# Attention and two expert layers on one core: how value products and row sums are laid out on TensorE's columns

## The chip, the cores and the metric

The kernel runs on one core of one Trainium2 chip. Its engines are called PE (TensorE; PEld is its weight load), DVE (VectorE), ACT (ScalarE), POOL (GpSimd) and SP (SyncE, which issues the DMAs here). The metric is the device time of one execution in microseconds (us); a number of runs gives a median.

## The reference

Three stages follow each other. Attention over 2 batches, 8 heads, 768 positions and head size 64; a key takes part for a query only where both fall into the same of 64 buckets, which the signs of six projections give:

```
mask = q_bucket[:, :, :, None] == k_bucket[:, :, None, :]
scores = where(mask, scale * (q @ k.T), -1e9)
attn = exp(scores - max(scores))
attn = attn / (sum(attn) + 1e-9)
out = attn @ v
```

Then a feed-forward layer with Mish over 1536 tokens (512 to 2048 to 512), and then eight experts of width 1024, whose weights per token come from a softmax balanced by eight Sinkhorn rounds. Everything is float32. The change touches only the attention stage.

## The kernel before

Work in attention is cut into 32 units `u`, one for each head and half of its queries (384 of 768). A unit has six chunks `c` of 128 keys. Its steps:

- `s_mm` multiplies queries by keys, two matmuls for each of three groups of 128 queries, and `s_max` (DVE) takes the row maxima. `rows_mm` turns them into a row, which `rows_cp` and a DMA (`rows_move`) put beside the queries.
- `st_mm` makes the transposed scores of one chunk with two matmuls (lines 414 and 415), and `st_exp` (ACT, line 420) writes their exponentials into one of five tiles `p` (128 keys x 384 queries).
- `av_mm` (line 458) multiplies `p` by the values of this chunk. The stationary operand has 128 columns: 64 of values and 64 of ones, so one output tile `pav` holds the unnormalised output on 64 partitions and the sums on the other 64. Two columns more than 384 (`WIDE`) carry a tiny constant for rows without a match.
- A chunk is multiplied in one of two ways. In plain float32 it is one matmul in the program, which the trace shows as two PE instructions (`pav<-p,vt`). A *split* chunk goes through the rounded type fp32r: `split_hi` (ACT or DVE, line 423) rounds `p` into `ph`, `split_lo` (POOL, line 426) makes the rest `pl`, and three matmuls follow (`ph,vl`, `pl,vh`, `ph,vh`). Chunks 0, 1 and 3 of each unit but the first are split: 93 split chunks and 99 plain ones.
- `av_out` moves sums (DVE transpose, line 466) and output (ACT copy, line 468) out of PSUM, and `norm` divides two heads together and rounds the result into `xh` and `xl`, the input of the next stage.
- `bits_mm` (line 343) computes the projections of a head. It is the one place where matmuls stand on column groups: four matmuls of 32 output columns each write PSUM partitions 0, 32, 64 and 96. Head 0 alone uses two groups of 64 columns.

No engine's order is written by hand. A planner takes tasks with costs (`COST`), due times and dependences, gives each engine (`E` is PE, `A` ACT, `D` DVE, `P` POOL, `Q` the DMA queue) its next task by the earliest start plus a small weight on the due time, and emits the code in that order. While PE would idle at the start it adds filler matmuls (`keep_warm`).

The first steps of the later stage, the decoding of the int64 weights, are woven into attention on ACT, DVE and POOL. The feed-forward layer begins with line 796.

Of the kernel before, what the change touches and what calls it, by code (L numbers as in the profile page):

```python
# [16 lines left out]
P = 128  # L17
# [5 lines left out]
E = 8  # L23
# [8 lines left out]
TINY = float(2.0 ** -64)  # L32
# [4 lines left out]
NS = 3  # L37
NRAW = 1
NP = 5
NPH = 3  # L40
# [3 lines left out]
WHOLE = {0: (0, 1, 3, 4), **{u: (4,) for u in range(1, 32)}}  # L44
# [20 lines left out]
def lsh_attention_moe_kernel(  # L65
# [111 lines left out]
    def attention():  # L177
        with ExitStack() as a:
# [14 lines left out]
            homes = {(NH - 3 + x) % NS: x for x in range(NX)}  # L193
# [8 lines left out]
            vt = [sets.tile([P, NKC, 3, D], F32, name=f"vt{i}") for i in range(2)]  # L202

            SPLIT = [0, 1, 3, 4]
            splits = lambda u, c: c in SPLIT and c not in WHOLE.get(u, ())
            vh = [sets.tile([P, len(SPLIT), 3, D], F32R, name=f"vh{i}") for i in range(2)]
            vl = [sets.tile([P, len(SPLIT), 3, D], F32R, name=f"vl{i}") for i in range(2)]
# [3 lines left out]
            some = out_p.tile([P, HALF // 32], F32, name="some")  # L211
# [4 lines left out]
            phs, pls = ([p_p.tile([P, 512], F32R, name=f"{n}{i}") for i in range(NPH)] for n in ("ph", "pl"))  # L216
# [3 lines left out]
            row_t, s_t, st_t, p_t, ph_t, av_t = {}, {}, {}, {}, {}, {}  # L220

            split_order = [(u, c) for u in range(NU) for c in range(NKC) if splits(u, c)]
            parts_no = {x: n for n, x in enumerate(split_order)}
            used_m = [0]
# [25 lines left out]
            def load_v(h):  # L250
                nc.sync.dma_start(out=vt[h // 2 % 2][:, :, h % 2 * 2, :], in_=v[h])

            def clear(kind, i):
                e = nc.vector if (kind, i) in FAST else nc.gpsimd
                if kind == "sq":
                    e.memset(f32(sq[i][64:96]), 0.0)
                elif kind == "bk":
                    e.memset(f32(bk[i][64:96]), 0.0)
                elif kind == "one":
                    e.memset(f32(bk[i][96:97]), 1.0)  # L260
                elif kind == "vt":
                    e.memset(vt[i][:, :, 1, :], 1.0)
                elif kind == "vl":
                    e.memset(f32(vl[i])[:, :, 1, :], 0.0)
                elif kind == "vh":
                    e.memset(f32(vh[i])[:, :, 1, :], 1.0)

            def clear_slots(j):
                t, x = ((ps, TINY), (phs, TINY), (pls, 0.0))[j]
                for y in t:  # L270
                    nc.gpsimd.memset((f32(y) if j else y)[:, HALF:WIDE], x)
# [11 lines left out]
            def keep_warm(n):  # L283
                if nm(av_mm, 1, 0) in ends:
                    return
                if nm(st_mm, 0, 0) in ends and len(warm) == 1:
                    if nm(av_mm, 0, 0) in ends:
# [73 lines left out]
            def queries(u):  # L361
                half = u % 2
                return slice(half * HALF, (half + 1) * HALF)

            def s_mm(u, t):
                s, q0 = u // 2 % NS, u % 2 * HALF + t * P
# [31 lines left out]
            def rows_cp(u):  # L398
                m = row_t[u]
                n = 1 if u < DIRECT else 3  # L400
                if u < DIRECT:
                    dst, src = sq[u // 2 % NS][96:97, queries(u)], m[0:n, :HALF]
# [5 lines left out]
            def rows_move(u):  # L408
                move(sq[u // 2 % NS][96:97, queries(u)], row_t[u])

            def st_mm(u, c):
                s, q, k = u // 2 % NS, queries(u), slice(c * P, (c + 1) * P)
# [15 lines left out]
            def split_hi(u, c, e):  # L428
                ph_t[u, c] = phs[parts_no[u, c] % NPH]
                copy(e, ph_t[u, c][:, :HALF], p_t[u, c][:, :HALF])  # L430

            def split_lo(u, c, e):
                lo = pls[parts_no[u, c] % NPH]
                subtract(e, lo[:, :HALF], p_t[u, c][:, :HALF], f32(ph_t[u, c])[:, :HALF])
                p_t[u, c] = lo

            def split_v(h, j, e):
                b = h // 2 % 2
                src = vt[b][:, :, h % 2 * 2, :].rearrange("p (a b) d -> p a b d", b=3)[:, :, 0:2]
                hi, lo = (x[b][:, :, h % 2 * 2, :].rearrange("p (a b) d -> p a b d", b=2) for x in (vh, vl))  # L440
                if j == 0:
                    copy(e, hi, src)
                else:
                    subtract(e, lo, src, hi.bitcast(F32))

            def av_mm(u, c):
                h = u // 2
                b, k = h // 2 % 2, slice(h % 2, h % 2 + 2)
                p = p_t.pop((u, c))
                if c == 0:  # L450
                    av_t[u] = slot(ps_a, "a", u, 2, [P, 512], F32, "pav")
                if splits(u, c):
                    i, hi = SPLIT.index(c), ph_t.pop((u, c))
                    pairs = [(vl[b][:, i, k], hi), (vh[b][:, i, k], p), (vh[b][:, i, k], hi)]
                else:
                    pairs = [(vt[b][:, c, k], p)]
                for n, (x, y) in enumerate(pairs):
                    nc.tensor.matmul(  # L458
                        av_t[u][:, :WIDE], x.rearrange("p a d -> p (a d)"), y[:, :WIDE],
                        start=(c == n == 0), stop=(c == NKC - 1 and n == len(pairs) - 1),  # L460
                    )

            def av_out(u, j):
                q, t, o = queries(u), av_t[u], 64 * (u // 2 % 2)
                if j == 0:
                    nc.vector.transpose(out=rs[o:o + 64, q], in_=t[64 - o:128 - o, :HALF])
                else:
                    nc.scalar.copy(xu[o:o + 64, u % 2, :WIDE], t[o:o + 64, :WIDE])


            def norm(u, part, e=None):
                h, half = divmod(u, 2)
                b, hp = divmod(h // 2, H // 2)
                c, x = queries(u), xu[:, half, :HALF]
                g = slice(b * S + half * HALF, b * S + (half + 1) * HALF)
                if part == 0:
                    nc.gpsimd.tensor_scalar(
                        out=some, in0=rs[:, c].rearrange("p (b j) -> p b j", j=32)[:, :, 0],
                        scalar1=0.0, scalar2=1e-9, op0=ALU.is_gt, op1=ALU.mult,
                    )  # L480
                elif part == 1:
                    nc.vector.scalar_tensor_tensor(
                        out=nr, in0=rs[:, c].rearrange("p (b j) -> p b j", j=32)[:, :, 0],
                        scalar=S * TINY, in1=some, op0=ALU.max, op1=ALU.add,
                    )
                    nc.vector.reciprocal(out=nr, in_=nr)
                elif part == 2:
# [4 lines left out]
                elif part == 3:  # L492
                    nc.vector.scalar_tensor_tensor(
                        out=x, in0=x, scalar=xu[:, half, HALF:HALF + 1], in1=rs[:, c], op0=ALU.add, op1=ALU.mult
                    )
                elif part == 4:
# [7 lines left out]
            def task(engines, due, f, *args, after=(), cost=None, lag=0.01, ring=None, frees=None):  # L504
# [3 lines left out]
                "E": dict(warm_up=2.6, bits_mm=0.66, s_mm=0.355, rows_mm=0.13, st_mm=0.355),  # L508
                "A": dict(
                    av_out=0.47, load_table=0.2, prep_hi=0.83, prep_move=0.83, st_exp=0.49,  # L510
                    split_hi=0.51, split_v=0.4, norm=0.51, decode=0.68, weight_hi=1.05,
                ),
                "D": dict(
                    av_out=0.58, bits_cmp=0.47, clear=0.7, clear_start=0.85, proj_parts=0.7, gate_parts=0.45,
                    prep_lo=0.64, s_max=0.95, rows_cp=0.29, split_hi=0.5, split_v=0.42,
                    norm=0.6, decode=0.46,
                ),
                "P": dict(
                    clear=0.6, prep_lo=1.0, split_lo=1.0, split_v=0.73, norm=1.0, decode=1.3, weight_lo=1.27,
                ),  # L520
            }
            SHARED = {prep_lo, proj_parts, split_hi, split_v, decode, clear, clear_start, gate_parts}
# [3 lines left out]
            PICK = (prep_lo, split_hi, split_lo, split_v, norm, decode)  # L526
# [3 lines left out]
            def st_done(u):  # L530
                return [nm(st_mm, u, c) for c in range(NKC)] if u >= 0 else []

# [9 lines left out]
            for j in range(3):  # L542
                task("P", -20 + j, clear_slots, j, cost=0.18)
# [5 lines left out]
            for i in range(2):  # L549
                for kind in ("vt", "vh", "vl"):  # L550
                    task("P", -3 + 2 * i, clear, kind, i, after=[nm(hold)])


            for h in range(NH):
                due = 6 * (2 * h - 3)
                old = 2 * (h - NS) + 1
# [28 lines left out]
                prev = h - 4  # L585
                freed = [nm(av_mm, 2 * prev + 1, NKC - 1), nm(split_v, prev, 1)] if prev >= 0 else []
                vdue = 12 * h - 12 * (h % 2) - 10.0
# [745 lines left out]
```

## Time and profile before

| | us |
|---|---|
| median of 3 runs | 1512.87 (1512.62 to 1513.23) |
| span of the profiled execution | 1511.8 |
| PE busy in the span | 1503.5 |
| first matmul of the feed-forward layer | 246.16 |

The span is what the instructions of the profiled execution cover; its own time is not given beside it, and the median of the runs is 1.1 us longer. A timeline gives the start of each PE instruction and its length. PE instructions are pipelined: one of 384 columns is shown as 0.34 us long, while the next one starts 0.18 us after it. So what a matmul costs a full PE is read from start to start, not from its length. The trace merges equal instructions that follow each other (x2), and the granted clock of PE is 1.00 in all slices.

### The profile page before, as it was taken

The numbers are of one execution on the slowest core, as the hardware profiler recorded it, in microseconds if no ns is written. First come the engines' busy times: TensorE is split into PE (matmuls) and PEld (weight loads), VectorE is DVE, ScalarE is ACT, GpSimd is POOL, SyncE is SP. The second block draws the span as 40 slices with busy tenths as digits, with TensorE's granted clock in tenths as the row PEclk, the third lists the DMA queues.
The fourth block names the chain that finished last, engine by engine and source line by source line (L and its number), as shares of the span: only waits on it lengthen the run. The fifth ranks groups of instructions, "written<-read, shape, count | busy, mean of one in ns | idle before, by whom it ended". The sixth has DMA issues, their size and how long they took to land.

```text
span 1511.8 us, 20162 instructions
## 1 busy us (share of the span) xinstructions
PE 1503.5 (99%) x7435; PEld 1318.3 (87%) x7435; DVE 885.7 (59%) x1419; ACT 685.6 (45%) x1225; POOL 902.8 (60%) x759
## 2 busy tenths in 40 slices
PE   9999999999999999999999999999999999999998
PEld 6788888888887898999989899998989999898988
DVE  7999896777625567666444466753434535344353
ACT  6778776654333343344333334343333434333331
POOL 5778774443313586666666666666666666666660
PEclk9999999999999999999999999999999999999999
DMA  8455641222200131222222222232222222222211
GB/s 217 118 156 147 146 111 29 84 84 70 70 14 3 41 97 59 68 70 70 70 70 70 63 64 70 70 110 71 70 68 61 67 70 70 70 70 70 64 49 42
DMA packets 66490, 116.70 MB, mean 77 GB/s; under 512 B 18276, under 2 KB 20440, under 8 KB 66392
## 3 DMA queue, kind: packets, MB, share of 16 engines
q1 hardware_dynamic: 66392, 115.43, 25.8%
q8 instruction: 58, 0.95, 0.3%
q14 instruction: 40, 0.33, 0.1%
HBM read 93.41 MB, written 3.15 MB: 64 GB/s over the span
## 4 chain that ended last, share of the span: by engine, by line
PE 97%; DVE 2%; issue 0%; ACT 0%; DVEq 0%; ACTq 0%
PE y L1185 35%; PE u L1118 31%; PE y L821 9%; PE pav L458 7%; PE h L796 3%; PE h L797 3%; PE h L798 3%; PE ps L372 2%; PE pst L414 2%; PE pst L415 2%; DVE mx L386 1%; PE pbits L343 0%; PE lg L849 0%; PE warm L291 0%; PE prow L395 0%
## 5 line engine op out<-in xcount | busy, mean ns | idle before, releaser
L1126 ACT ACTIVATE gh<-c 128x384 fp32r<-128x384 f32 x256 | 134.6, 526 | 174.6 <-DVE c L1138 172.6
L1138 DVE TENSOR_TENSOR u<-u,p 128x384 f32<-128x384 f32 x64 | 35.7, 558 | 284.1 <-PE u L1118 282.2
L1131 DVE SCALAR_TENSOR_TENSOR gl<-c,gh 128x384 fp32r<-128x384 f32 x256 | 195.7, 827 | 0.0
L1185 PE MATMUL y<-ww,gh 128*128 128x512 f32 x768 | 186.6, 391 | 0.0
L1185 PE MATMUL y<-w,gh 128*128 128x512 f32 x768 | 186.0, 391 | 0.0
L1185 PEld LDWEIGHTS y<-w,gh 128*128 128x128 f32 x768 | 143.7, 188 | 28.9
L1185 PEld LDWEIGHTS y<-ww,gh 128*128 128x128 f32 x768 | 143.7, 188 | 28.8
L1001 POOL TENSOR_TENSOR w<-stage,w 128x1024 fp32r<-128x1024 f32 x32 | 76.3, 2386 | 89.1 <-ACT w L997 89.1
L426 POOL TENSOR_TENSOR pl<-p,ph 128x384 fp32r<-128x384 f32 x93 | 99.5, 1079 | 44.7 <-ACT ph L423 41.7
L1001 POOL TENSOR_TENSOR ww<-stage,ww 128x1024 fp32r<-128x1024 f32 x32 | 76.3, 2384 | 81.7 <-ACT ww L997 81.7
L420 ACT ACTIVATE p<-pst 128x384 f32<-128x384 f32 x192 | 93.5, 490 | 49.4 <-PE pav L458 26.5
L821 PE MATMUL y<-gh,w 128*128 128x512 f32 x336 | 109.8, 389 | 0.0
L151 POOL TENSOR_TENSOR stage<-stage,sgn 128x512 f32<-128x512 f32 x32 | 43.1, 1347 | 110.4 <-DVE sgn L149 100.4
L997 ACT CAST ww<-stage 128x1024 fp32r<-128x1024 f32 x32 | 33.6, 1052 | 157.5 <-PE y L1185 157.5
L997 ACT CAST w<-stage 128x1024 fp32r<-128x1024 f32 x32 | 33.6, 1050 | 154.5 <-PE y L1185 154.5
L386 DVE TENSOR_REDUCE mx<-ps 128x1 f32<-128x768 f32 x95 | 90.1, 949 | 18.8 <-PE ps L372 17.9
L977 POOL TENSOR_TENSOR wa<-stage,wa 128x512 fp32r<-128x512 f32 x32 | 45.6, 1424 | 89.0 <-ACT wa L972 80.0
L1185 PE MATMUL y<-ww,gl 128*128 128x512 f32 x384 | 98.2, 389 | 0.0
L1185 PE MATMUL y<-w,gl 128*128 128x512 f32 x384 | 97.6, 389 | 0.0
L977 POOL TENSOR_TENSOR wx<-stage,wx 128x512 fp32r<-128x512 f32 x32 | 45.4, 1419 | 80.5 <-ACT wx L972 80.5
L1118 PE MATMUL u<-tw,w 128*128 128x384 f32 x480 | 91.9, 336 | 0.0
L1118 PE MATMUL u<-tw,ws 128*128 128x384 f32 x480 | 91.7, 336 | 0.0
(218 smaller groups left out, 3843.4 us busy)
## 6 DMA issues: line engine op xcount, KB each, us to landing
stage<-in_w_dram SPq DMA_DIRECT2D x160, 512.0 KB
raw<-in_qk_dram SPq DMA_DIRECT2D x13, 384.0 KB
sb<-hi SPq DMA_DIRECT2D x18, 192.0 KB
vt<-in_v_dram SPq DMA_DIRECT2D x16, 192.0 KB
wx<-hi SPq DMA_DIRECT2D x16, 192.0 KB
out_dram<-acc SPq DMA_DIRECT2D x11, 256.0 KB
zq<-hi SPq DMA_DIRECT2D x10, 192.0 KB
ak<-hi SPq DMA_DIRECT2D x10, 192.0 KB
```

The costliest lines, as they stand in the source:

```text
L386: nc.vector.tensor_reduce(out=m[:, t:t + 1], in_=s_t[t][:, :, :HALF], axis=AX.XY, op=ALU.max, negate=True)
L420: nc.scalar.activation(p_t[u, c][:, :HALF], st_t.pop((u, c))[:, :HALF], AF.Exp, scale=0.125)
L426: (nc.gpsimd if e == "P" else nc.vector).tensor_sub(out, in0, in1)
L458: nc.tensor.matmul(av_t[u][:, :WIDE], x.rearrange("p a d -> p (a d)"), y[:, :WIDE], start=(c == n == 0), stop=(c == NKC - 1 and n == len(p ...
L821: nc.tensor.matmul(yps[j], x, y, start=(head and m == 0), stop=(tail and m == 2))
L977: nc.gpsimd.tensor_sub(a[:, 1, 0:512], t[:, 0, :], f32(a)[:, 0, 0:512])
L997: nc.scalar.copy(wbuf[u % 2]["w"][:, 0, :], staged["u", u, 1].rearrange("p c n -> p (c n)"))
L1001: nc.gpsimd.tensor_sub(y[:, 1, :], t, f32(y)[:, 0, :])
L1118: nc.tensor.matmul(bank[x], weight(u, a, m, kc), moving(u, b, mm, kc), start=(first and n == 0), stop=(n == 5), skip_group_check=not first)
L1126: nc.scalar.activation(hi, src, AF.Relu)
L1131: nc.vector.scalar_tensor_tensor(out=lo, in0=src, scalar=0.0, in1=f32(hid_u[u, c][0]), op0=ALU.max, op1=ALU.subtract)
L1185: nc.tensor.matmul(y_t[t], (hi, hi, lo)[m][:, t % 3 * P:(t % 3 + 1) * P], y, start=(k == 0 and first), stop=(k == NF // 2 - 1 and last),)
```

## The change

Both ways of multiplying a chunk are replaced by one. Heads 2k and 2k+1 are now handled together: `members(n)` names the two units of a pair, which have the same half of the queries, and for the first four units the order of heads and halves is changed (`head`, `half_of`). `av_mm` issues, for one chunk, two float32 matmuls with 64 stationary columns (values alone): the even head writes PSUM partitions 0 to 63, the odd head 64 to 127. For the first two pairs each unit's chunk is a task of its own (`av_one`).

The sums no longer come with the values. POOL adds chunks 0 and 1, and 2 and 3, of a unit (`add`), and `sum_mm` multiplies these sums and chunks 4 and 5 by ones, eight float32 matmuls of 32 output columns on four column groups for a pair. Each head's sum then lies in two parts on two partition groups; `norm` brings them together with an ACT copy and four small DMAs. `split_hi`, `split_lo`, `split_v` and `av_out` go. There are 14 tiles `p` in place of 5, a fourth set of operands (`NS`), and six tiles `pa`.

```diff
-NS = 3
-NP = 5
-NPH = 3
-WHOLE = {0: (0, 1, 3, 4), **{u: (4,) for u in range(1, 32)}}
+NS = 4
+NP = 14
+NPA = 6
+AVG = 1
+AVX = 0.1
+AVD = 6
+ADDS = "P"
...
-                if splits(u, c):
-                    i, hi = SPLIT.index(c), ph_t.pop((u, c))
-                    pairs = [(vl[b][:, i, k], hi), (vh[b][:, i, k], p), (vh[b][:, i, k], hi)]
-                else:
-                    pairs = [(vt[b][:, c, k], p)]
...
+            def add(u, g, e):
+                t = pa_t[u, g] = pas[(2 * u + g) % NPA]
+                (nc.gpsimd if e == "P" else nc.vector).tensor_add(t, p_t[u, 2 * g][:, :HALF], p_t[u, 2 * g + 1][:, :HALF])
+
+            def av_chunks(n, us, g):
+                if n not in av_t:
+                    av_t[n] = slot(ps_a, "a", n, 2, [P, 512], F32, "pav")
+                for c in range(AVG * g, AVG * g + AVG):
+                    for u in us:
+                        e = head(u) % 2
+                        nc.tensor.matmul(
+                            av_t[n][64 * e:64 * e + 64, :WIDE], vt[head(u) // 2 % 2][:, c, e, :], p_t[u, c][:, :WIDE],
+                            start=(c == 0), stop=(c == NKC - 1),
+                        )
...
+            def sum_mm(n):
+                sum_t[n] = next_m("psum")
+                for k in range(2):
+                    for u in members(n):
+                        for x in range(2):
+                            r = 64 * (head(u) % 2) + 32 * x
+                            nc.tensor.matmul(
+                                sum_t[n][r:r + 32, :HALF], ones[:, 0:32], p_t[u, 4 + x][:, :HALF] if k else pa_t[u, x],
+                                start=(k == 0), stop=(k == 1),
+                            )
+
+            def norm_move(n, x):
+                y = x ^ 1
+                nc.sync.dma_start(out=other[32 * x:32 * x + 32], in_=own[32 * y:32 * y + 32])
...
-                    task("E", i + 1.0, av_mm, u, c, cost=0.53 if sp else 0.65,
...
+                        task("E", 6 * part[-1] + AVG * g + AVD, f, x, g,
+                             after=[nm(st_exp, u, c) for u in part for c in range(AVG * g, AVG * g + AVG)] + ([nm(f, x, g - 1)] if g else room)
...
+                task("E", due + 8, sum_mm, n, after=[nm(add, u, g) for u in us for g in range(2)] + [nm(st_exp, u, c) for u in us for c in (4, 5)], ring="m", frees=nm(norm, n, 0))
...
+                    task("Q", due, norm_move, n, x, lag=0.3, after=[nm(norm, n, 1)])
```

On PE the planner's order is a new one throughout. In the middle of attention of the kernel before, between the score matmuls (`ps`, `pst`), PE has one matmul of a plain chunk and three of a split one, all with 128 output partitions (the numbers behind a name are those of buffers):

```order
L414 MATMUL pst<-wx_78 128x384
L415 MATMUL pst<-wx_78 128x384
L458 MATMUL pav<-p_140,vt_125 128x386
L458 MATMUL pav<-ph_141,vl_129 128x386
L458 MATMUL pav<-pl_144,vh_127 128x386
L458 MATMUL pav<-ph_141,vh_127 128x386
L414 MATMUL pst<-wx_78 128x384
L415 MATMUL pst<-wx_78 128x384
```

In the kernel after, PE has there two matmuls of 64 output partitions, one for each head of a pair, alone between score matmuls of 128:

```order
L442 MATMUL pav<-p_137,vt_128 64x386
L442 MATMUL pav<-p_143,vt_128 64x386
L399 MATMUL prow<-idt,mx_157 3x128
L376 MATMUL ps<-wx_78 128x384 x2
L418 MATMUL pst<-wx_78 128x384
L419 MATMUL pst<-wx_78 128x384
L418 MATMUL pst<-wx_78 128x384
L419 MATMUL pst<-wx_78 128x384
L442 MATMUL pav<-p_138,vt_128 64x386
L442 MATMUL pav<-p_144,vt_128 64x386
```

A few rows on, the sums of an earlier pair stand on PE, also between score matmuls:

```order
L419 MATMUL pst<-wx_78 128x384
L459 MATMUL psum<-pa_154,ones 32x384
L459 MATMUL psum<-pa_155,ones 32x384
L459 MATMUL psum<-pa_150,ones 32x384
L459 MATMUL psum<-pa_151,ones 32x384
L459 MATMUL psum<-p_140,ones 32x384
L459 MATMUL psum<-p_141,ones 32x384
L459 MATMUL psum<-p_146,ones 32x384
L459 MATMUL psum<-p_147,ones 32x384
L418 MATMUL pst<-wx_78 128x384
```

So the value products have moved from whole-width instructions among others of the same width to narrow ones. In the whole program of the kernel after they stand in 96 runs of neighbouring `pav` matmuls: 71 runs with one matmul on each of the two groups, 5 with two chunks and one with three chunks in a row on both groups, and 19 runs on one group only (14 single matmuls and 5 of two, all from the first two pairs). `psum` stands 16 times, `pbits` 16 times as before. In 12 places two of these narrow runs touch.

## Rows read from the trace of the kernel before

**Rows 1.** The page: busy time, and the chain that ended last.
```profile
PE 1503.5 (99%) x7435; PEld 1318.3 (87%) x7435; DVE 885.7 (59%) x1419; ACT 685.6 (45%) x1225; POOL 902.8 (60%) x759
...
PE 97%; DVE 2%; issue 0%; ACT 0%; DVEq 0%; ACTq 0%
PE y L1185 35%; PE u L1118 31%; PE y L821 9%; PE pav L458 7%; PE h L796 3%; PE h L797 3%; PE h L798 3%; PE ps L372 2%; PE pst L414 2%; PE pst L415 2%; DVE mx L386 1%; PE pbits L343 0%; PE lg L849 0%; PE warm L291 0%; PE prow L395 0%
```

**Rows 2.** Windows: stretch, its length, busy time and instructions of each engine, clock, DMA.
```profile
0.00:60.00 60.00, 55.84 (x294) 42.87 (x295) 47.54 (x79) 40.48 (x78) 34.89 (x58) 1.00 0.67 172
60.00:200.00 140.00, 139.69 (x745) 116.36 (x744) 126.49 (x192) 107.98 (x228) 106.81 (x108) 1.00 0.59 150
```

**Rows 3.** Timeline of PE, mid-attention: start, length, instruction, count.
```profile
152.66 0.34 PE L415 MATMUL pst<-sb 97*128 97x384 f32 x1
152.84 0.81 PE L458 MATMUL pav<-p,vt 128*128 128x386 f32 x2
153.19 0.63 PE L458 MATMUL pav<-ph,vl 128*128 128x386 f32 x1
153.66 0.34 PE L458 MATMUL pav<-pl,vh 128*128 128x386 f32 x1
153.84 0.33 PE L458 MATMUL pav<-ph,vh 128*128 128x386 f32 x1
154.01 0.34 PE L414 MATMUL pst<-zq,ak 128*128 128x384 f32 x1
```

**Rows 4.** Lines by shape to 247 us, PE: count, busy time, mean length in ns.
```profile
L458 PE MATMUL pav<-p,vt 128*128 128x386 f32 x198 | 80.0, 486 | 0.0
L458 PE MATMUL pav<-ph,vl 128*128 128x386 f32 x93 | 40.7, 437 | 0.0
L343 PE MATMUL pbits<-raw,pf 128*32 128x192 f32 x104 | 6.9, 338 | 0.0
L291 PE MATMUL warm<-xh 128*128 128x256 f32 x45 | 6.9, 292 | 0.0
```

**Rows 5.** Timeline of PE around one group of four narrow matmuls (eight instructions).
```profile
15.18 0.34 PE L414 MATMUL pst<-zq,ak 128*128 128x384 f32 x1
15.35 0.33 PE L415 MATMUL pst<-sb 97*128 97x384 f32 x1
15.62 0.53 PE L343 MATMUL pbits<-raw,pf 128*32 128x192 f32 x8
16.08 0.62 PE L372 MATMUL ps<-sb 96*128 96x384 f32 x2
16.53 0.34 PE L414 MATMUL pst<-zq,ak 128*128 128x384 f32 x1
```

**Rows 6.** Timeline of PE at its start: head 0's two groups of 64.
```profile
3.04 0.63 PE L281 MATMUL warm<-xh 128*128 128x512 f32 x1
...
3.46 0.63 PE L281 MATMUL warm<-xh 128*128 128x512 f32 x1
4.02 1.80 PE L343 MATMUL pbits<-raw,pf 128*64 128x384 f32 x4
5.76 0.58 PE L291 MATMUL warm<-xh 128*128 128x256 f32 x1
```

**Rows 7.** Timeline of PE: narrow matmuls on the first group alone.
```profile
466.57 0.39 PE L821 MATMUL y<-gh,w 128*128 128x512 f32 x1
466.79 1.10 PE L849 MATMUL lg<-xh,wgr 128*32 128x512 f32 x4
467.73 1.08 PE L849 MATMUL lg<-xl,wgr 128*32 128x512 f32 x4
468.64 0.40 PE L796 MATMUL h<-xh,wx 128*128 128x512 f32 x1
```

**Rows 8.** Lines by shape to 247 us, the other engines.
```profile
L426 POOL TENSOR_TENSOR pl<-p,ph 128x384 fp32r<-128x384 f32 x93 | 99.5, 1079 | 44.7 <-ACT ph L423 41.7 <-PE pav L458 1.8 <-DVE ph L423 0.7
...
L423 ACT CAST ph<-p 128x384 fp32r<-128x384 f32 x81 | 41.5, 513 | 2.4
```

**Rows 9.** Timeline of PE at the end of attention.
```profile
245.16 1.46 PE L458 MATMUL pav<-p,vt 128*128 128x386 f32 x4
246.16 0.69 PE L796 MATMUL h<-xh,w 128*128 128x512 f32 x1
```

More of the change, by code (lines that the diff above doesn't have):

```diff
@@ L191, in attention @@
             NU = 2 * NH
-            homes = {(NH - 3 + x) % NS: x for x in range(NX)}
+            homes = {(NH - NS + x) % NS: x for x in range(NX)}
             def part(i, j, name):
@@ L201, in attention @@
             ak = [part(i, 3, f"ak{i}") for i in range(NS)]
[L202 to L207, printed above, removed]
+            vt = [sets.tile([P, NKC, 2, D], F32, name=f"vt{i}") for i in range(2)]
             xu = out_p.tile([P, 2, 512], F32, name="xu")
@@ L210, in attention @@
             nr = out_p.tile([P, HALF // 32], F32, name="nr")
-            some = out_p.tile([P, HALF // 32], F32, name="some")
+            own, other = (out_p.tile([P, HALF // 32], F32, name=n) for n in ("own", "other"))
             pj = out_p.tile([P, 12], F32, name="pj")
@@ L215, in attention @@
             ps = [p_p.tile([P, 512], F32, name=f"p{i}") for i in range(NP)]
-            phs, pls = ([p_p.tile([P, 512], F32R, name=f"{n}{i}") for i in range(NPH)] for n in ("ph", "pl"))
+            pas = [p_p.tile([P, HALF], F32, name=f"pa{i}") for i in range(NPA)]
             warm = []
@@ L219, in attention, with head, half_of, pair_of @@
             mx_t = [out_p.tile([P, 4], F32, name=f"mx{i}") for i in range(2)]
-            row_t, s_t, st_t, p_t, ph_t, av_t = {}, {}, {}, {}, {}, {}
-            split_order = [(u, c) for u in range(NU) for c in range(NKC) if splits(u, c)]
-            parts_no = {x: n for n, x in enumerate(split_order)}
+            row_t, s_t, st_t, p_t, pa_t, av_t, sum_t = {}, {}, {}, {}, {}, {}, {}
             used_m = [0]
+            def head(u):
+                return u // 2 if u < 4 else 2 * (u // 4) + u % 2
+            def half_of(u):
+                return u % 2 if u < 4 else u // 2 % 2
+            def pair_of(u):
+                return u % 2 if u < 4 else u // 2
+            def members(n):
+                return (n, n + 2) if n < 2 else (2 * n, 2 * n + 1)
+            def uses(h):
+                return [u for u in range(NU) if head(u) == h]
             def slot(pool, tag, i, n, shape, dtype, name):
@@ L258, in clear @@
                     e.memset(f32(bk[i][64:96]), 0.0)
[L259 removed]
+                else:
                     e.memset(f32(bk[i][96:97]), 1.0)
[L261 to L266, printed above, removed]
             def clear_slots(j):
[L269 to L271 removed]
+                for y in ps[j::2]:
+                    nc.gpsimd.memset(y[:, HALF:WIDE], TINY)
             def clear_start():
@@ L475, in norm @@
+            def norm_move(n, x):
+                y = x ^ 1
+                nc.sync.dma_start(out=other[32 * x:32 * x + 32], in_=own[32 * y:32 * y + 32])
+            def norm(n, part, e=None):
+                hp, half = divmod(n, 2)
+                b, hp = divmod(hp, H // 2)
+                c, x = slice(half * HALF, (half + 1) * HALF), xu[:, half, :HALF]
                 g = slice(b * S + half * HALF, b * S + (half + 1) * HALF)
+                first = rs[:, c].rearrange("p (b j) -> p b j", j=32)[:, :, 0]
@@ L476, in norm @@
                 if part == 0:
[L477 to L480, printed above, removed]
+                    nc.vector.transpose(out=rs[:, c], in_=sum_t[n][:, :HALF])
                 elif part == 1:
[L482 to L485, printed above, removed]
+                    nc.scalar.copy(own, first)
+                elif part == 3:
+                    nc.vector.scalar_tensor_tensor(out=nr, in0=other, scalar=EPS, in1=own, op0=ALU.add, op1=ALU.add)
@@ L491, in norm @@
                     )
-                elif part == 3:
+                elif part == 5:
                     nc.vector.scalar_tensor_tensor(
-                        out=x, in0=x, scalar=xu[:, half, HALF:HALF + 1], in1=rs[:, c], op0=ALU.add, op1=ALU.mult
+                        out=x, in0=av_t[n][:, :HALF], scalar=av_t[n][:, HALF:HALF + 1], in1=rs[:, c], op0=ALU.add, op1=ALU.mult
                     )
-                elif part == 4:
+                elif part == 6:
                     copy(e, xh[:, hp, g], x)
@@ L541, in attention @@
             task("D", -8, proj_parts, after=[nm(clear_start), nm(load_const, 0)])
-            for j in range(3):
-                task("P", -20 + j, clear_slots, j, cost=0.18)
+            for j in range(2):
+                task("P", -20 + j, clear_slots, j, cost=0.35)
             task("D", 20, gate_parts, after=[nm(load_const, 3)])
@@ L548, in attention @@
                     task(e, -8.5 + 3 * i + n / 4, clear, kind, i, after=[nm(clear, "bk", i)] * (n == 2) + [nm(hold)] * (i > 0))
-            for i in range(2):
-                for kind in ("vt", "vh", "vl"):
-                    task("P", -3 + 2 * i, clear, kind, i, after=[nm(hold)])
             for h in range(NH):
-                due = 6 * (2 * h - 3)
-                old = 2 * (h - NS) + 1
+                due = 6 * (uses(h)[0] - 3)
+                old = uses(h - NS)[1] if h >= NS else -1
                 shared = [h for h in range(NH) if h not in (1, 2, *AHEAD)]
@@ L599, in attention @@
                     task("E", due + 2 * t, s_mm, u, t,
-                         after=[nm(prep_move, h, 0), nm(prep_move, h, 1), *([nm(bits_move, h, x) for x in range(4)] if h else [nm(bits_cmp, 0, *x) for x in ((0, 1), (1, 1), (u, 0))])] + [before] * (u > 0 or t > 1))
+                         after=[nm(prep_move, h, 0), nm(prep_move, h, 1), *([nm(bits_move, h, x) for x in range(4)] if h else [nm(bits_cmp, 0, *x) for x in ((0, 1), (1, 1), (half, 0))])] + [before] * (u > 0 or t > 1))
                     task("D", due + 2 * t + 0.5, s_max, u, t, after=[nm(s_mm, u, t)] + [nm(rows_mm, u - 2)] * (t == 0 and u > 1))
@@ L623, in attention @@
-                pair = u - 4
-                read = [nm(norm, pair + (1 - h % 2) * 2, 4), nm(norm, pair + (1 - h % 2) * 2, 5)] if h > 1 else [nm(bits_mm, x) for x in (1, 2)] + [nm(prep_lo, x, i) for x in (1, 2) for i in range(2)]
-                for j in range(2):
-                    task("DA"[j], 6 * u + 10.0 + j / 2, av_out, u, j,
-                         after=[nm(av_mm, u, NKC - 1)] + read)
-                if h % 2:
-                    both = [nm(av_out, x, j) for x in (u - 2, u) for j in range(2)]
-                    due = 6 * u + 14.0
-                    task("P", due, norm, u, 0, cost=0.27, after=both + ([nm(norm, u - 1 if half else u - 3, 2)] if u > 3 or half else []))
-                    task("D", due, norm, u, 1, cost=0.47, after=[nm(norm, u, 0)])
-                    task("D", due, norm, u, 2, cost=0.58, after=[nm(norm, u, 1)])
-                    task("D", due, norm, u, 3, cost=0.72, after=[nm(norm, u, 2)])
-                    task("A" if u < NU - 1 else "D", due + 2, norm, u, 4, after=[nm(norm, u, 3)])
-                    task("PD" if u < NU - 1 else "D", due + 3, norm, u, 5, after=[nm(norm, u, 4)])
+                    read = [av_done(old[0], old[1] // AVG), nm(add, old[0], old[1] // 2) if old[1] < 4 else nm(sum_mm, pair_of(old[0]))] if old else []
```

127 lines of the change are left out of this document (54 added, 73 removed).

## The prediction, made before the changed kernel ran

> **What bounds the kernel now.** I read the page first, for the engine that sets the end, and then windows and timelines of the attention stage, the only one that changes. The page says that PE is busy for 99% of the span and that 97% of the chain that ended last is PE [rows 1]. Busy time of pipelined instructions overstates, so the windows come next: from 60 to 200 us PE is busy 139.69 of 140.00 us, while DVE, the next, has 126.49 [rows 2]. The timeline settles it: in mid-attention each PE instruction starts 0.17 to 0.18 us after the one before, or later by its own extra work, without a hole [rows 3]. At the end of attention the last value products are followed by the feed-forward layer's first matmul at 246.16 us, without a hole either [rows 9]. So in attention time is PE's issue time, and the change is worth what it adds and removes there. In the first 60 us PE has 4.16 us of idle time (60.00 less 55.84) and 45 filler matmuls [rows 2, 4]; only there can added work hide.
>
> **What goes.** From 152.84 to 153.66 us stand one plain chunk and the first matmul of a split one, 0.82 us; the next two starts are 0.18 and 0.17 us apart [rows 3]. So a split chunk costs 3 x 0.176 = 0.53 us and a plain one 0.82 - 0.176 = 0.645 us. There are 93 split chunks, and 198/2 = 99 plain ones [rows 4]. Removed: 93 x 0.53 + 99 x 0.645 = 49.1 + 63.9 = 113.0 us of PE. The splits on POOL (93 x 1.08 us) and ACT (81 x 0.51 us) go too [rows 8], but PE waits for neither, so I count nothing for them.
>
> **What comes, if column groups run side by side.** Four groups do: eight instructions of 192 columns start at 15.62 and the next instruction starts at 16.08, 0.46 us [rows 5]. A float32 instruction of 386 columns takes 0.645/2 = 0.32 us, so one of 192 takes 0.16, and eight in turn would take 1.28 us; two rounds of four at once take 0.32. For two groups of 64 there is one sample, at half the clock: there fillers of 512 columns start 0.42 us apart [rows 6], which is 1.2 GHz. At that rate one instruction of 384 columns in float32 takes 0.64 us, four in turn 2.56, two rounds of two 1.28; from 4.02 to 5.76 it took 1.74 [rows 6]. So two groups also run together, with something on top.
> From the runs that the order shows: 71 + 5 x 2 + 3 = 84 chunks of two heads in one turn each, and 14 + 5 x 2 = 24 chunks of one head, together 108 turns x 0.645 = 69.7 us. A sum is eight matmuls on four groups, two rounds of two instructions: 4 x 0.32 = 1.28 us, x 16 = 20.5 us. The pure work falls by 113.0 - 69.7 - 20.5 = 22.8 us.
>
> **What a change of layout costs.** This decides. From the `pst` at 15.35 to the one at 16.53 pass 1.18 us [rows 5]. In it lie three ordinary matmuls (the first `pst` and two `ps`), 3 x 0.176 = 0.53, and the four-group work of 0.32. The other 0.33 us are nobody's work: 0.09 before (15.62 less 15.35, less 0.176), 0.14 inside, 0.10 after (0.45 for two `ps` in place of 0.35). PE waited for no other engine there, and the other heads' groups show the same 0.46 us. A whole-width float32 chunk among fp32r ones shows nothing of the kind [rows 3], so it is the groups and not the type. The sample of two groups keeps 1.74 - 1.28 = 0.46 us on top inside alone at half the clock, so it isn't spared either; part of that can be a wait for the second half of its data.
> The Trainium skill says in "TensorEngine Tiling (Array Packing)", section "Tiling Modes", that changing the tiling mode, not just the tile, drains the engine; by that rule each run of narrow matmuls between wide ones pays, and the 0.33 us above agree with it.
> Before, 16 runs were narrow. After it is 96 + 16 + 16 = 128, of which 12 touch another narrow run, so 116 changes in place of 16: 100 x 0.34 = 34 us (0.33 and 0.01 for the wider weight load of 64 columns). For the 12 contacts, where two kinds of narrow layout meet, I take 0.2 us each, 2.4 us, between 0 and 0.34. The 19 runs on one group alone may be free: eight narrow matmuls on the first group alone begin 0.22 us after a wide one and the next wide one begins 0.23 us after the last, as wide ones do (466.57 to 466.79, and 467.73 to 468.64 is 0.91 for four) [rows 7]. These are on the first group in one type, ours are of another type and ten of them on the second group, so I take half: 19 x 0.34 / 2 = 3.2 us off, between 0 and 6.5. The first pairs, where the 24 chunks of one head stand, also fall in the stretch with idle PE: 2 us off, between 0 and 4.
>
> **Other engines.** POOL gets 64 `add`s; its nearest row, a subtraction of the same shape, takes 1.08 us [rows 8], so 69 us for the 99.5 that go. ACT and DVE lose more than they get (a reduction, transposes and products per pair in place of per head). Four small DMAs per pair are added on the SP queue, behind an ACT copy. While they wait the next heads' loads and rows queue behind them, but those are issued a unit or more ahead of PE's need; their cover is PE's own 14 us per pair, and if it fails the wait shows up under the second rival. The trace of before has no such DMA, so between 0 and 1 us per pair; I take 0.
>
> **The sum.** -22.8 + 34 + 2.4 - 3.2 - 2 = +8.4 us. On the profiled execution's span of 1511.8 us that is 1520.2, and the median of before is 1.1 us above that span, so **1521.3 us**. With the free ends of all terms (contacts 0, lone runs free, 4 us hidden) it is -22.8 + 34 - 6.5 - 4 = +0.7; with the dear ends +15.3 (contacts 0.34, the rest paid). So this forecast's own range is 1513.6 to 1528.2.
>
> **Rivals.** *The change of layout is nearly free for two groups.* Then only the 16 sums pay, 16 x 0.34 = 5.4 us, and the two-group runs cost 0 to 0.1 us each (0.1 is the planner's own extra for a chunk, `AVX`): -22.8 + 5.4 + 0 to 9.6 = -17.4 to -7.8 us, 1495.5 to 1505. For it: lone groups show no loss [rows 7], and two groups have only a slow and disturbed sample [rows 6]. Against it: all four-group runs pay, and the sample keeps a rest that work doesn't explain. The point from which it decides: the 22.8 us are used up when a change costs 0.26 us ((22.8 - 2.4 + 3.2 + 2) / 100); below that the kernel is faster.
> The skill's "TensorE: Matmul & The Clock Gate", section "Measured speedup vs the span model", gives matmuls on different groups as one matmul's time and about 4 ns for each further tile, with nothing for getting in and out; by this alone no run pays, the sums neither, and the time would be 1490. There [rows 5] do not agree: 0.46 us stand where it gives 0.33.
> *New waits.* Tiles `p` are held longer: a pair's chunk needs both heads' exponentials, and chunks 4 and 5 wait for the sums, which wait for POOL. If PE waits once per pair for one add (1.08 us [rows 8]), that is 14 to 16 x 1.08 = 15 to 17 us on top of the 8.4: 1536 to 1539. Against it: POOL has 30 us less to do, and PE's slower turn gives it time. It needs holes on PE, of which there are none now [rows 2].
> *The groups do not run side by side.* Then 84 x 0.645 = 54 us and 16 x 3.84 = 61 us come on top: over 1630 us. Rows 5 and 6 exclude nearly all of it.
>
> **How the numbers follow.** The forecast gets 0.69, free changes 0.18, waits 0.11, no overlap 0.02. About 0.2%, 3 us, is what a measurement of this kernel can tell from no change. Faster by more: the first rival, and hardly anything of the forecast, 0.18. Within: the lower tenth of the forecast, 0.09. Slower: 0.73. The range of 8 in 10 takes the forecast's own, goes up half of the way to the second rival, whose waits may come in part of the pairs, and down to the slow edge of the first: 1504 to 1533.
>
> **What would show it.** In the changed kernel's timeline a pair's four `pav` instructions should take about 0.8 us to the next start, with that start's successor 0.1 us late, and 0.09 us before them: 0.99 in all where pure work is 0.645. A `psum` should take 1.6 us. The feed-forward layer should begin near 254.5 us, and what follows should take as long as before (1265.6 us from 246.16 to the end). I am wrong in mechanism if a pair of `pav` takes under 0.8 us in all, or if PE shows holes with a releaser on ACT, POOL or a DMA.

## The result, and the profile after

The changed kernel takes 1524.01 us (median of 4 runs, 1523.54 to 1525.96) where the kernel before takes 1512.86 (4 runs): a ratio of 1.0076 with an interval of 1.0061 to 1.0090, slower by 11.2 us. Predicted were 1521.3 us and slower; the time lies in the forecast's own range.

First the page of the kernel after, which answers to [rows 1]: busy time, and the chain that ended last.

```profile
span 1522.2 us, 20364 instructions
PE 1514.4 (99%) x7583; PEld 1252.4 (82%) x7583; DVE 853.5 (56%) x1387; ACT 630.8 (41%) x1113; POOL 853.3 (56%) x701
...
PE 98%; DVE 1%; DMA 1%; SPq 0%; issue 0%; ACT 0%; POOL 0%; DVEq 0%; ACTq 0%
```

PE still sets the end, and the other engines are less busy than before. Its windows answer to [rows 2]:

```profile
0.00:60.00 60.00, 57.05 (x279) 30.60 (x280) 40.52 (x69) 29.30 (x55) 28.75 (x49) 1.00 0.75 180
60.00:200.00 140.00, 139.62 (x815) 74.50 (x814) 106.63 (x176) 73.98 (x156) 75.71 (x71) 1.00 0.62 152
```

From 60 to 200 us PE is as full as before (139.62 of 140.00 us), and DVE, ACT and POOL are busy for 20, 34 and 31 us less. So the stage is longer by PE's own instructions, not by waits. Where attention ends, in PE's timeline, answers to [rows 9]:

```profile
256.54 0.50 PE L790 MATMUL h<-xh,w 128*128 128x512 f32 x1
```

That is 10.4 us later than the 246.16 of before, nearly all of the loss; the rest of the kernel takes 1265.6 us in both. The time of this execution is 1.8 us above its span. The 1.1 us given for before is the median of some executions less the span of another; where both are listed for one execution of the kernel before (beside the experiments below), its time too is 1.7 to 1.8 us above its span. So the other 0.7 us of the 11.2 come from that pairing, and are not shown to be a cost of the change.

The place on which the prediction rests, in PE's timeline, against [rows 3, 5]:

```profile
153.91 0.33 PE L419 MATMUL pst<-wx 97*128 97x384 f32 x1
154.17 0.87 PE L442 MATMUL pav<-p,vt 128*64 128x386 f32 x4
154.97 0.62 PE L376 MATMUL ps<-sb 96*128 96x384 f32 x2
155.43 0.34 PE L418 MATMUL pst<-wx 128*128 128x384 f32 x1
...
155.96 0.34 PE L419 MATMUL pst<-wx 97*128 97x384 f32 x1
156.22 0.85 PE L459 MATMUL psum<-pa,ones 128*32 128x384 f32 x8
156.89 0.83 PE L459 MATMUL psum<-p,ones 128*32 128x384 f32 x8
157.65 0.62 PE L376 MATMUL ps<-sb 96*128 96x384 f32 x2
158.11 0.34 PE L418 MATMUL pst<-wx 128*128 128x384 f32 x1
```

The four instructions of a pair begin 0.26 us after the wide matmul ahead of them (0.18 is ordinary), take 0.80 us, and the two wide ones behind take 0.46 in place of 0.35. So 0.645 us of work cost 0.08 + 0.80 + 0.11 = 0.99 us, as the prediction has it, and a sum costs 0.08 + 1.43 + 0.11 = 1.62.

Two more places of the same timeline show terms that the prediction had to guess: matmuls on one group alone (the first two rows of `pav`, with the wide matmul ahead of them: one head, two instructions, and then two in a row on the same group), and a place where narrow runs touch.

```profile
22.64 0.34 PE L419 MATMUL pst<-wx 97*128 97x384 f32 x1
22.91 0.86 PE L442 MATMUL pav<-p,vt 128*64 128x386 f32 x2
23.70 0.62 PE L376 MATMUL ps<-sb 96*128 96x384 f32 x2
24.25 1.51 PE L442 MATMUL pav<-p,vt 128*64 128x386 f32 x4
...
159.90 0.53 PE L347 MATMUL pbits<-raw,pf 128*32 128x192 f32 x8
160.37 1.52 PE L442 MATMUL pav<-p,vt 128*64 128x386 f32 x8
161.81 0.62 PE L376 MATMUL ps<-sb 96*128 96x384 f32 x2
```

One head alone takes 0.79 us from 22.91 to 23.70, as long as two side by side; it begins 0.27 us after the wide matmul ahead of it, and the two `ps` behind it take so long (0.55 us to the next narrow run) that both the way in and the way out are paid: it isn't spared. Where `pbits` and `pav` touch, the way out and in falls away, and only the rest inside remains: two chunks take 1.44 us, 2 x 0.645 + 0.15.

### The profile page after: what moved, and what is told of

It is laid out like the page before. It is cut to its first block, busy times and chain, and to the rows that moved or that the text cites. A ratio compares the mean times of both kernels' runs of the same rounds, so it can differ in the third digit from the quotient of the medians.

```text
span 1522.2 us, 20364 instructions
## 1 busy us (share of the span) xinstructions
PE 1514.4 (99%) x7583; PEld 1252.4 (82%) x7583; DVE 853.5 (56%) x1387; ACT 630.8 (41%) x1113; POOL 853.3 (56%) x701
## 4 chain that ended last, share of the span: by engine, by line
PE 98%; DVE 1%; DMA 1%; SPq 0%; issue 0%; ACT 0%; POOL 0%; DVEq 0%; ACTq 0%
PE y L1179 34%; PE u L1112 31%; PE y L815 9%; PE pav L442 5%; PE pst L418 3%; PE h L792 3%; PE h L790 3%; PE h L791 3%; PE ps L376 2%; PE pst L419 2%; PE psum L459 1%; PE pbits L347 1%; DMA raw<-in_qk_dram 0%; PE lg L843 0%; PE prow L399 0%
## 5 line engine op out<-in xcount | busy, mean ns | idle before, releaser
L424 ACT ACTIVATE p<-pst 128x384 f32<-128x384 f32 x192 | 89.8, 490 | 110.9 <-PE pst L419 66.4
L434 POOL TENSOR_TENSOR pa<-p,p 128x384 f32<-128x384 f32 x64 | 65.3, 1021 | 90.8 <-ACT p L424 90.6
L442 PE MATMUL pav<-p,vt 128*64 128x386 f32 x384 | 91.1, 510 | 0.0
```

The costliest lines, as they stand in the source:

```text
L424: nc.scalar.activation(p_t[u, c][:, :HALF], st_t.pop((u, c))[:, :HALF], AF.Exp, scale=0.125)
L434: (nc.gpsimd if e == "P" else nc.vector).tensor_add(t, p_t[u, 2 * g][:, :HALF], p_t[u, 2 * g + 1][:, :HALF])
L442: nc.tensor.matmul(av_t[n][64 * e:64 * e + 64, :WIDE], vt[head(u) // 2 % 2][:, c, e, :], p_t[u, c][:, :WIDE], start=(c == 0), stop=(c == N ...
```

## The experiments

**Is it the number of runs?** The theory (1) is that each run of narrow matmuls between wide ones costs PE about 0.35 us, and that nothing else was lost. Then fewer, longer runs give the time back. The rivals: the order was planned with costs that are too low, and PE waits (2); narrow matmuls are slow however they stand (3); longer runs are given back as waits (4). The changed kernel has two numbers for this, the chunks in a task (`AVG`) and the planner's extra for one (`AVX`); the cost that the planner has for a sum was raised as well. The diff writes the four kernels in one.

```diff
-AVG = 1
-AVX = 0.1
+AVG = 1, 2, 3 or 6
+AVX = 0.35
...
-sum_mm=1.5
+sum_mm=1.62
```

Expected with `AVG` 1 (e1_costs): 

> The planner is told what a change of layout costs: 0.35 us on each chunk in place of 0.1, 1.62 us for a sum in place of 1.5; the kernel is otherwise the changed one. Its order has 103 runs of value products where the changed kernel has 96, and 10 places where two narrow runs touch in place of 12. Theory 1 (each run of narrow matmuls costs PE 0.35 us, 0.19 us less where it touches another, and nothing else was lost): +2.8 us against the changed kernel, about 1526.8. Theory 2 (the changed kernel lost time to waits, because its order was planned with costs that were too low): faster than the changed kernel, 1515 to 1522.

With 2 (e2_two): 

> Two chunks in each task, so that four or eight narrow matmuls follow each other; 54 runs of value products in place of 96, the same matmuls. Theory 1 (0.35 us for each run): 42 runs fewer and 7 touching places fewer, -14.5 + 1.3 = -13.2 us against the changed kernel, about 1510.8. Theory 3 (the narrow matmuls are slow in themselves, 0.99 us for each chunk of two heads however they stand): no change, 1524. Theory 4 (longer runs hold the tiles of exponentials longer and PE waits for them): the runs are fewer but holes show up on PE, 1515 to 1525.

With 3 (e3_three): 

> Three chunks in each task; 36 runs of value products in place of 96. Theory 1: 60 runs fewer, 7 touching places fewer, -20.8 + 1.3 = -19.5 us, about 1504.5, below the kernel before (1512.9). Theory 3: no change, 1524. Theory 4: holes on PE with ACT as releaser, 1510 to 1525.

With 6 (e4_six): 

> All six chunks of a pair in one task; 18 runs of value products in place of 96. Theory 1 alone: 78 runs fewer and 10 touching places fewer, -27.0 + 1.9 = -25.1 us, about 1499. Theory 4: twelve of the fourteen tiles of exponentials are held until a run of 4.2 us begins, so PE waits for ACT around each run; with about 1 us for each of 14 pairs 1510 to 1515, more if it is 2 us.

Measured, with the ratio to the kernel before (1513.63 us in these runs):

| | runs of `pav` | by the count of runs | measured us | ratio (interval) |
|---|---|---|---|---|
| e1_costs | 103 | 1526.8 | 1537.89 | 1.0165 (1.0141 to 1.0189) |
| e2_two | 54 | 1510.8 | 1534.40 | 1.0138 (1.0123 to 1.0153) |
| e3_three | 36 | 1504.5 | 1530.35 | 1.0115 (1.0098 to 1.0132) |
| e4_six | 18 | 1499 | 1549.31 | 1.0244 (1.0225 to 1.0262) |

None came out as the count of runs has it, and all are slower than the changed kernel. Theory 2 falls: the changed kernel has next to no waits to lose (its list stands below), and told the true costs the planner made a slower order. In e1_costs, in the profiled execution, attention ends at 266.43 us, 9.9 us after the changed kernel's; 2.8 us of this is the count of runs, and PE is idle for 7.0 us up to there in place of 3.3, mostly for DVE's maxima. The rest stays open. The runs themselves obey theory 1, not 3; PE's timeline of e3_three:

```profile
136.30 0.44 PE L418 MATMUL pst<-zq,ak 128*128 128x384 f32 x1
...
137.10 0.45 PE L418 MATMUL pst<-zq,ak 128*128 128x384 f32 x1 [0.18 <-ACT p L424]
...
138.65 0.34 PE L419 MATMUL pst<-sb 97*128 97x384 f32 x1
138.93 2.17 PE L442 MATMUL pav<-p,vt 128*64 128x386 f32 x12
141.02 0.62 PE L376 MATMUL ps<-sb 96*128 96x384 f32 x2
141.48 0.34 PE L418 MATMUL pst<-wx 128*128 128x384 f32 x1
```

Three chunks take 2.09 us, 3 x 0.645 + 0.15, with 0.10 us before and 0.11 behind: one charge for three. But ahead of the run two score matmuls that take 0.35 us elsewhere take 0.80 (136.30 to 137.10), because ACT is not ready. Only 0.18 of the 0.45 lost is shown as a wait. The trace counts a wait from the end of the matmul ahead, which is 0.34 us long, where the next one ordinarily starts after 0.18; and the weights of a matmul that waited are loaded late too, so that the one behind it starts after 0.28 us (136.30 to 136.58). ACT's timeline of the same kernel shows why:

```profile
137.83 0.94 ACT L424 ACTIVATE p<-pst 128x384 f32<-128x384 f32 x2 [0.32 <-PE pst L419]
...
139.09 0.49 ACT L424 ACTIVATE p<-pst 128x384 f32<-128x384 f32 x1
142.09 0.87 ACT L424 ACTIVATE p<-pst 128x384 f32<-128x384 f32 x2 [2.51 <-PE pst L419]
```

While PE is in the run ACT has one exponential left and then sits idle for 2.51 us, until the first `pst` after the run: the program has only two `pst` tiles to hold scores ahead. Then PE must feed ACT again and is held up by it, as ahead of this run. PE's waits up to the end of attention, of the kernel after and then of e3_three and e2_two (who waited for whom, us in total, times, longest):

```profile
...
PE ps L376 <- DVE mx L390: 0.5, 1, 0.5
PE pst L418 <- ACT p L424: 0.4, 2, 0.2
```

```profile
PE pst L418 <- ACT p L424: 6.4, 24, 0.4
PE pst L419 <- DMA sb<-row: 2.7, 2, 1.5
PE ps L376 <- DVE mx L390: 2.0, 4, 0.7
...
```

```profile
PE pst L419 <- DMA sb<-row: 4.5, 3, 2.0
PE pst L418 <- ACT p L424: 3.8, 15, 0.3
...
```

So longer runs bring waits, as theory 4 has it, but not by the way that it names. ACT hardly waits for a value product to free a tile of exponentials (1.2 us up to 280 us in e3_three, 1.4 in e2_two, 27.8 in the changed kernel). PE waits for ACT to free a `pst`, in these orders also for the row that a DMA brings late, and in e4_six most of all for DVE's maxima (5.7 us from 20 to 250 us, for ACT 5.0).

How much of the loss these waits are, the traces show in part. In e2_two, e3_three and e4_six attention ends at 264.83, 262.18 and 279.02 us, in place of 256.54. That is 21, 25 and 48 us above the count of runs. Up to there PE is idle for 15.1, 14.9 and 24.4 us, in the changed kernel for 3.3, so the added idle time is about half of it. The other half was not separated. In it are what each wait costs beside its idle time, as in the rows above, and a lowered clock, which the count of runs leaves out: the granted clock is 0.93 from 200 to 250 us in e2_two, 0.97 from 150 to 200 us in e3_three and 0.93 from 60 to 200 us in e4_six, where both kernels have 1.00. By these figures the clock costs at most 3.5, 1.5 and 9.8 us, an estimate (the missing share times the stretch).

**Can a better order keep the saving?** e9_two_ordered takes e2_two and sets the due times of the planner's tasks and their weight (`DELTA`) anew; `DUE0` and `PACE` are the due times of the later stage's decoding.

```diff
-AVD = 6
-DELTA = 0.012
-DUE0 = 45
-PACE = 21
+AVD = 1.5
+DELTA = 0.0207
+DUE0 = 60
+PACE = 22
...
-                due = 6 * u - 16.0
+                due = 6 * u - 19.0
...
-                    task("E", i - 4.0, st_mm, u, c,
+                    task("E", i - 6.5, st_mm, u, c,
...
-                    task("A", i - 9.0, st_exp, u, c,
+                    task("A", i - 3.5, st_exp, u, c,
...
-                task("E", due + 8, sum_mm, n,
+                task("E", due + 0.5, sum_mm, n,
```

The due times of `add` (22 in place of 3) and `norm` (4.5 in place of 10) moved as well.

> Two chunks in each task as in e2_two, and the due times of the planner's tasks set anew, so that by the planner's own account PE waits less; 54 runs of value products, 2 places where narrow runs touch. Theory 1 with theory 4 (a change of layout costs 0.35 us; what e2_two lost beside was waits that its order made): the pure count gives 1524.0 - 42 x 0.346 + 10 x 0.19 = 1511.4 without waits; with a third to a half of the 18 to 24 us that e2_two lost to waits 1517 to 1523, in any case 8 us or more below e2_two (1534.4). Rival (longer narrow runs make the waits, whatever the order): within 4 us of 1534.

Measured: 1525.10 us (ratio 1.0074, 1.0059 to 1.0089). With the same 54 runs that is 9.3 us below e2_two, so order and not run length made those 9.3; but it is above the 1517 to 1523 expected, and no faster than the changed kernel (1524.01 in its own runs). Its waits of PE:

```profile
PE pst L418 <- ACT p L424: 4.4, 12, 1.5
...
```

The late rows are gone, the waits for ACT are not. PE is idle for 9.5 us up to the end of attention, and the granted clock is 0.97 from 100 to 150 us. Attention ends at 256.25 us, 0.3 us before the changed kernel's, but what follows takes 1.8 us longer than there. Whether more `pst` tiles would end them wasn't tried.

**The disputed cost by itself.** Four kernels put one or two nearly empty matmuls into the kernel *before*, ahead of the score matmuls of 95 groups of queries. They write columns of the score tile that nothing reads. The diff is that of e5_empty_two.

```diff
                     s_t[t] = ps_s.tile([P, 2, 512], F32, tag="s", name="ps")
+                    for o in (0, 64):
+                        nc.tensor.matmul(
+                            s_t[t][o:o + 64, 0, 400:416], sq[s][0:96, q0:q0 + 64].bitcast(F32), bk[s][0:96, 0:16].bitcast(F32), start=True, stop=True,
+                        )
```

e6_empty_one keeps the first group alone (`(0,)`), e7_empty_one_r does the same in type fp32r (no bitcast), e8_empty_wide uses all 128 columns in float32.

e5_empty_two: 

> The kernel before, with two added float32 matmuls of 64 output columns on the two column groups, 16 moving columns each, ahead of the score matmuls of each group of 128 queries (95 places; they write columns of PSUM that nothing reads). This prices a change of layout with nearly no work in it. Theory 1 (each narrow run between wide ones costs about 0.09 us to get in, 0.05 for weights, 0.09 to drain and 0.1 to get out, and here a second weight load): 0.33 to 0.40 us each, less some places in the first 45 us that hide it, +29 to +38 us, 1542 to 1551. Rival (narrow matmuls are just instructions in the stream, as 4 ns for each further tile would have it): four instructions of at most 0.05 us, +5 to +20 us, 1518 to 1533.

e6_empty_one: 

> As the run on two groups, but one float32 matmul on the first group alone. Theory 1 as the changed kernel's trace has it (runs on one group cost as much as runs on two): the same +29 to +38 us. Rival (a run on the first group alone is free, as the later stage's narrow matmuls of type fp32r are): +5 to +12 us, 1518 to 1525.

e7_empty_one_r: 

> As the run on one group, but in type fp32r (one instruction in place of two). If the type decides (fp32r on the first group is no change of layout, as the later stage's rows suggest): 95 instructions of 0.06 to 0.1 us, +4 to +10 us, 1517 to 1523. If the group width decides: +25 to +38 us.

e8_empty_wide: 

> Control: the added matmul in float32 with all 128 output columns, 16 moving columns, two instructions and no change of layout. Both theories: two weight loads of 128 columns, 0.11 to 0.18 us each, +18 to +33 us at most if they bound PE, less where they are loaded during the matmul before; 1523 to 1546. What theory 1 needs is that the narrow ones cost more than this by the drains, although they load half as many columns.

Measured against 1513.23 us: e5_empty_two 1546.64 (ratio 1.0221, 1.0192 to 1.0251), e6_empty_one 1545.71 (1.0215, 1.0185 to 1.0245), e7_empty_one_r 1522.63 (1.0063, 1.0040 to 1.0086), e8_empty_wide 1531.88 (1.0124, 1.0094 to 1.0153). Divided by 95 that is 0.35, 0.34, 0.10 and 0.20 us for each. All four lie in a span given before: e5 and e6 in that of theory 1 and not of its rival, e7 in that of "the type decides", e8 in the one that both theories share. The same place in PE's timeline, a plain chunk and two `ps` up to the next `pst`: first the kernel before, without the added matmul, then e5 to e8 in turn.

```profile
156.06 0.81 PE L458 MATMUL pav<-p,vt 128*128 128x386 f32 x2
156.41 0.81 PE L372 MATMUL ps<-wx 96*128 96x384 f32 x2
157.06 0.34 PE L414 MATMUL pst<-zq,ak 128*128 128x384 f32 x1
```

```profile
152.14 0.81 PE L462 MATMUL pav<-p,vt 128*128 128x386 f32 x2
152.88 0.29 PE L372 MATMUL ps<-sb 96*64 96x16 f32 x4
153.10 0.62 PE L376 MATMUL ps<-sb 96*128 96x384 f32 x2
153.56 0.34 PE L418 MATMUL pst<-zq,ak 128*128 128x384 f32 x1
```

```profile
151.79 0.81 PE L462 MATMUL pav<-p,vt 128*128 128x386 f32 x2
152.54 0.29 PE L372 MATMUL ps<-sb 96*64 96x16 f32 x2
152.75 0.62 PE L376 MATMUL ps<-sb 96*128 96x384 f32 x2
153.21 0.34 PE L418 MATMUL pst<-zq,ak 128*128 128x384 f32 x1
```

```profile
154.46 0.81 PE L462 MATMUL pav<-p,vt 128*128 128x386 f32 x2
154.81 0.47 PE L372 MATMUL ps<-wx 96*64 96x16 f32 x1
155.13 0.59 PE L376 MATMUL ps<-wx 96*128 96x384 f32 x2
155.56 0.34 PE L418 MATMUL pst<-zq,ak 128*128 128x384 f32 x1
```

```profile
151.87 0.81 PE L462 MATMUL pav<-p,vt 128*128 128x386 f32 x2
152.52 0.29 PE L372 MATMUL ps<-sb 96*128 96x16 f32 x2
152.66 0.60 PE L376 MATMUL ps<-sb 96*128 96x384 f32 x2
153.11 0.34 PE L418 MATMUL pst<-zq,ak 128*128 128x384 f32 x1
```

From the first start to the last: 1.00 us without it, 1.42, 1.42, 1.10 and 1.24 with it. Two things follow.

First, a float32 run in narrow form costs 0.42 us with next to no work in it, on one group as on two. But 0.24 of this is what an empty wide matmul costs at the same place: behind it too the two `ps` take 0.45 us, where they take 0.46 behind the narrow ones. Only in the narrow forms does the run begin late (152.88 and 152.54, where the chunk's 0.645 us would let it begin 0.1 us sooner), and it is 0.07 us longer inside (0.22 and 0.21 in place of 0.14). By the times, the narrow form adds 0.16 and 0.15 us to the wide one at each place (e5 and e6 less e8, divided by 95). So these kernels show that the narrow form in float32 has a price of its own. That it is 0.35 us with work in the run is read in the changed kernel, beside wide chunks of the kernel before, which show nothing on top of their 0.645 us [rows 3].

Second, it is the narrow form in this type that costs, not the narrow form alone: in fp32r one group adds 0.10 us, about half of what the wide float32 matmul with its two instructions adds. The average of 0.35 is below 0.42, since in the first 60 us part of it fills holes and in some places the added run touches another narrow one; these two shares were not separated.

**The change against not splitting at all.** e10_plain is the kernel before with all chunks in plain float32.

```diff
-WHOLE = {0: (0, 1, 3, 4), **{u: (4,) for u in range(1, 32)}}
+WHOLE = {u: (0, 1, 3, 4) for u in range(32)}
```

> The kernel before with no chunk split: all 192 are one wide float32 matmul, with the ones beside the values; no narrow layout, no splitting, no added sums. 93 chunks x (0.645 - 0.53) = +10.7 us, 1523.6: the changed kernel's time, so that putting two heads side by side gains nothing over not splitting at all. If splits on POOL and ACT were holding the kernel before up, less: 1515 to 1520.

Measured: 1523.80 us against 1513.79 (ratio 1.0067, 1.0050 to 1.0084), 10.0 us more where 10.7 were expected. It confirms the difference between the prices of a split and a plain chunk, and that the splits hardly held PE up (at most 0.7 us). It is also the changed kernel's time: what two heads side by side save over 192 wide chunks, the layout changes and the sums take.

## Why the prediction was right, step by step

*What bounds.* PE's issue time: right, it stays full, and the loss stands in its own instructions.

*What goes.* e10_plain puts 10.0 us on the difference between plain and split for 93 chunks, where the prediction's prices give 10.7. The two prices themselves rest on [rows 3].

*The work side by side.* Right. A pair's four instructions take 0.80 us with everything, where two chunks in turn would take 1.29, and two pairs in a row 1.44 with one charge. (The sample at half the clock, head 0's groups, stands in a stretch for which the windows list a granted clock of 1.00. That it is half rests on the pace of the fillers alone, 0.42 us for 512 columns [rows 6] in place of 0.22 [rows 7].)

*The change of layout.* The deciding term was right in mechanism and size: 0.35 us for two groups in the changed kernel, where 0.34 was assumed, and the sum closes with it. That an empty run in the kernel before also costs 0.35 on the average is in part luck, since an empty wide one costs 0.20 there. The prediction's "it is the groups and not the type" is only half right: it takes both, a narrow form and float32 (e7_empty_one_r). The rule that changing the tiling mode drains the engine (the Trainium skill, "TensorEngine Tiling (Array Packing)", "Tiling Modes") agrees with e5_empty_two, 0.16 us dearer at each place than e8_empty_wide; it does not say why e7_empty_one_r is spared. The rule that counts 4 ns for a further tile (the Trainium skill, "TensorE: Matmul & The Clock Gate", "Measured speedup vs the span model") holds only between groups of one run, 0.80 us for two heads and 0.79 for one, and not for getting into it and out. The first rival falls with the 0.35 us of the changed kernel.

*Lone runs.* Wrong. The prediction took half of 19 x 0.34 off, by the rows of `lg` [rows 7]. Those are fp32r; the value products are float32, and a lone one pays in full (the rows at 22.91, and e6_empty_one, as dear as e5_empty_two). The term is 0, not -3.2.

*Contacts.* 0.2 us each was assumed, the trace has 0.15, so 1.8 us in place of 2.4.

*The start.* 2 us hidden were assumed. In the first 60 us PE is busy for 57.05 where it was 55.84, and 30 fillers stand where 45 did:

```profile
L295 PE MATMUL warm<-xh 128*128 128x256 f32 x30 | 5.2, 302 | 0.0
```

1.2 us of holes and 15 fillers of 0.12 us (1.8 us) make 3.0. The sum with the measured terms is -22.8 + 100 x 0.346 + 1.8 - 3.0 = +10.6 us, and the trace has +10.4. So forecast and trace differ by 2.0 us (+8.4 and +10.4): the lone runs add 3.2 and the price of a run 0.6, the start and the contacts take back 1.0 and 0.6, and 0.2 stays open. That the forecast came so close is in part this offset. The other 0.7 us between forecast and median are the pairing of a span with other executions' times, as said with the result.

*Other engines, and waits.* Right for the changed kernel: no wait of PE over 0.5 us behind its start. The four small DMAs per pair cost PE nothing that its waits show. The second rival did not decide here. In e2 to e4 and e9 waits did come, by another way than it names: not tiles `p` and POOL, but two `pst` tiles and ACT, late rows and DVE's maxima.

## What to carry to other kernels

Narrow float32 matmuls on column groups paid about a third of a microsecond here for each excursion between wide ones, with one group or with two; count the excursions in the order, not the matmuls, before counting on the overlap. Making the excursions longer moves the cost only if the other engines have buffers to work from during them: here, with two score tiles, ACT sat idle for 2.5 us around a run of 2.1 us. And before a new layout is built, the plain form without it is worth a run.

## What was not expected of the hardware

A single float32 matmul of 64 output columns on the first group costs as much to get in and out as two groups (0.42 us at the same place), while the same in fp32r adds 0.10 us and all 128 columns in float32 add 0.24; the runs do not show what in the type makes it so. And where PE has more holes, the granted clock is below 1.00 in places. Most of all in e4_six, 0.93 on the average from 60 to 200 us, so a mix of its two levels (1.2 and 2.4 GHz); both kernels have 1.00 there:

```profile
60.00:200.00 140.00, 127.81 (x726) 75.90 (x726) 97.92 (x155) 65.07 (x137) 63.93 (x59) 0.93 0.51 135
```

PE is busy for 127.81 of 140 us in that stretch (in the changed kernel for 139.62). So part of the loss of that kernel can be clock, on top of the waits; how much was not separated.
